# Gated mix of segment attention and SwiGLU: the logit fills of a quad in its own three visits, and pair loads issued 25 slots ahead from GpSimd's queue

## The chip, the cores and the metric

The kernel runs on one core of one Trainium2 chip. The metric is the device time of one execution in microseconds. A run of it was timed three times before the change, and one further execution was profiled; times inside the kernel are from that profile and count from the start of its span.

## The reference

The program mixes two branches over the same input x, 2048 rows of 640. Branch A is attention in 4 segments of 512 rows with 32 heads of 20 elements: causal softmax inside a segment, plus a read of a memory (the sum over the earlier segments of phi(k) times v), mixed per head by sigmoid(beta), and projected by wo. Branch B is a SwiGLU feed-forward with 1728 hidden columns. A gate per row mixes the two.

```
for s in range(4):                       # segments of 512 rows
    logits = einsum("bhqd,bhkd->bhqk", q[s], k[s]) * scale + causal_mask
    a_dot  = softmax(logits) @ v[s]
    a_mem  = (phi(q[s]) @ M) / (phi(q[s]) @ z + 1e-6)
    o      = sigmoid(beta) * a_mem + (1 - sigmoid(beta)) * a_dot
    M, z   = M + phi(k[s])^T @ v[s],  z + sum(phi(k[s]))
a = concat(o) @ wo
b = (silu(x @ w1) * (x @ w3)) @ w2
g = sigmoid(x @ gate_w)
return g * a + (1 - g) * b
```

The change is inside the softmax attention, in `logits` and what is needed to subtract each row's maximum.

## The kernel before

**How the attention is tiled.** Two neighbouring heads are a pair, two pairs (four heads) a quad. There are 4 segments x 32 heads = 128 heads, so 64 pairs and 32 quads. Queries and keys, split into a high and a low part so that fp32 precision is kept, are stored to DRAM (`qkd`), 60 rows for each head. `load_pair` (line 540) brings a pair back into one of four buffers `qk` (pair p uses buffer p % 4), each head by a DMA of 240 KB (line 549), head 0 in partitions 0 to 59, head 1 in 64 to 123. Rows 60 and 61 of each head are left for the maxima.

**Two passes over the logits.** A quad's logits are computed twice. The first pass (`s_fill`, line 564) has queries on the output's partitions; PE writes a bank of PSUM for each head of a pair, and DVE reduces each bank to row maxima in the tile `m` (line 579). The work of a quad is cut into five fills, numbered by the table `S_FILL`; fill 3 is the one whose bank holds a block of both pairs, fills 0 and 1 belong to the first pair, 2 and 4 to the second. Each table entry is (pair, block of queries, column in the bank):

```
    S_FILL = (((0, 3, 0),), ((0, 2, 0), (0, 0, 384)), ((1, 3, 0),), ((0, 1, 0), (1, 1, 256)), ((1, 2, 0), (1, 0, 384)))
    T_FILL = (((0, 0, 0),), ((0, 1, 0), (0, 3, 384)), ((0, 2, 0), (1, 2, 256)), ((1, 0, 0),), ((1, 1, 0), (1, 3, 384)))
```

`max_rows` (line 583) turns a quad's maxima into rows: ACT copies them (`ns`, line 139, and `nh`, line 140), DVE subtracts (line 141) and transposes them into `mr` (line 590), and four small DMAs from POOL's queue write `mr` into rows 60 and 61 of the four heads (line 595), those of the first pair ahead of those of the second. The second pass (`t_fill`, line 597) then computes the logits with keys on the partitions and 62 rows, so that the maxima are subtracted by the matmul itself; ACT takes the exponential (line 613) and POOL clears what lies above the diagonal (line 617). Fills t0 and t1 read the first pair, t2 both pairs, t3 and t4 the second pair. `pv_quad` (line 622) multiplies by v (line 627).

**Slots and visits.** The rest of the program (projections, feed-forward, output projection) is a stream of matmuls, woven with the attention by hand: `attention` (line 718) counts 40 slots for each quad, and between two slots as much of the stream is issued as its share asks for. At three slots of an iteration, named by `VISITS`, the fills are issued; an entry (kind, q, fill) of iteration m works on quad m - q. A visit at slot 5 of the next iteration is slot 45 counted from this one. `after(n, f)` runs f at the n-th slot from now. The second pass and the PV of a quad run in the next iteration and the one behind it.

**Who sets the order.** The order of PE is the program's own. On the other engines a scheduler orders the instructions, mostly as the program has them; calls wrapped in `here` stay where they are. An engine takes its instructions in order: one that waits for a semaphore holds up what is behind it on that engine, and a DMA's issue is such an instruction. Pair loads are issued by ACT, the maxima's DMAs by POOL, weights mostly by SP. POOL also takes part in splitting weights (W) and hidden tiles (ht), line 116.

Of the kernel before, what the change touches and what calls it, by code (L numbers as in the profile page):

```python
# [8 lines left out]
F32 = mybir.dt.float32  # L9
# [18 lines left out]
RH, LEAD = 3 * DH, 20  # L28
# [9 lines left out]
def gated_mix(ctx: ExitStack, tc: tile.TileContext, xT, wqk, wv, w13, w2, w2h, wo, beta, out):  # L38
    nc = tc.nc
# [6 lines left out]
    qkd = [dp.tile([3 * D, 2, L], F32, name=f"qkd{c}") for c in range(NSEG)]  # L46
# [54 lines left out]
    here = tc.keep_in_program_order  # L101
# [34 lines left out]
    def split_psum(dst, src, name, pin=lambda ins: ins):  # L136

        hi = bank_tile(name)[:, :src.shape[-1]]
        pin(nc.scalar.copy(dst[:, 0], src))
        nc.scalar.copy(hi, dst[:, 0].bitcast(F32))  # L140
        nc.vector.tensor_sub(dst[:, 1], src, hi)
# [301 lines left out]
    def job_read(c):  # L443
        return 5.6, memory_read(c)
# [95 lines left out]
    def load_pair(p):  # L540

        j = 2 * p
        c, h = divmod(j, H)
        t = qk[p % NST]
        for mb in {DH * h // P, (DH * h + 2 * DH - 1) // P}:
            assert ("q", c, mb) in stored and ("k", c, mb) in stored
        assert ("v", c, 3) in stored
        for i in range(2):
            here(nc.scalar.dma_start(t[64 * i:64 * i + RH].bitcast(F32), qkd[c][RH * (h + i):RH * (h + i + 1)]))
        if h % 8 == 0:  # L550
            bank["v"] = v = vg[j // 8 % NVG]
            here(nc.sync.dma_start(v[:, :, :VG], vd[c][:, :, VE * h:VE * h + VG]))
        if p % 2 == 0:
            bank["m"] = sp.tile([P, 16], F32, tag="m", name=f"m{j}", bufs=2)
        for i in range(2):
            o = VE * (h % 8 + i)
            heads[j + i] = dict(c=c, h=h + i, v=bank["v"][:, :, o:o + 32])
        pairs[p] = dict(t=t, m=bank["m"])
# [24 lines left out]
    def max_rows(p):  # L583

        m = pairs[p]["m"]
        ns = nsT[p // 2 % 2]
        split_psum(ns.rearrange("p (a n) -> p a n", a=2), m, f"nh{p}")
        mr = sp.tile([32, P], F32, tag="mr", name="mr", bufs=1)
        for g in range(4):
            nc.vector.transpose(mr[:, 32 * g:32 * g + 32], ns[32 * g:32 * g + 32].bitcast(F32))  # L590
        for k in range(2):
            for a in range(2):
                dst = pairs[p + k]["t"][RH + a:RH + a + 65:64, 0].rearrange("h (b n) -> h b n", n=P)
                r = 16 * a + 8 * k
                after(4 + 9 * k, lambda d=dst, r=r: here(nc.gpsimd.dma_start(d, mr[r:r + 8])))  # L595

    def t_fill(m, f):

# [23 lines left out]
    def pv_quad(p):  # L622

        ps = bank_tile(f"o{p}")
        for kb, (o, n) in enumerate(PSEG):
            for i in range(4):
                nc.tensor.matmul(ps[32 * i:32 * i + 32, kb * P:], heads[2 * p + i]["v"][:, kb],  # L627
                                 pairs[p + i // 2]["P"][:, i % 2, o:o + n],
                                 start=kb == 0, stop=kb == 3, skip_group_check=True)
        ot = sp.tile([P, L], F32, tag="oq", name=f"oq{p}", bufs=1)  # L630
        nc.scalar.copy(ot, ps)  # L631
        c, h = heads[2 * p]["c"], heads[2 * p]["h"]
        nc.scalar.dma_start(od[c][h:h + 4].rearrange("h e n -> (h e) n"), ot)
        q = p // 2 % 8
        for b in OUT.get(q, ()):
            after(8, o_load, c, b)
        if q == 7:
            after(6 if c < NSEG - 1 else 2, o_sums, c)
# [63 lines left out]
    def after(n, f, *a):  # L702
        soon.append([n, f, a])

    def tick():
        for e in list(soon):
            e[0] -= 1
            if e[0] <= 0:
                soon.remove(e)
                e[1](*e[2])  # L710

    NQUAD = NJ // 4


    VISITS = {5: (("s", 0, 3), ("s", 0, 1), ("o", 2), ("t", 1, 0), ("t", 1, 1)),
              18: (("s", 0, 2), ("t", 1, 2), ("s", 0, 4)), 31: (("s", -1, 0), ("t", 1, 3), ("t", 1, 4))}

    def attention():

        for m in range(-1, NQUAD + 2):  # L720
            for n in range(40):
                if m == -1 and n < 40 - LEAD:
                    continue
                if n in VISITS:
                    yield "visit"
                    for kind, q, *f in VISITS[n]:
                        if 0 <= m - q < NQUAD:
                            if kind == "o":
                                pv_quad(2 * (m - q))
                            else:  # L730
                                (s_fill if kind == "s" else t_fill)(m - q, *f)
                    if n == 18 and 0 <= m < NQUAD:
                        after(6, max_rows, 2 * m)
                elif n in (20, 32) and m + 1 < NQUAD:
                    load_pair(2 * (m + 1) + (n == 32))
                tick()
                yield m

# [62 lines left out]
    def job_down(cs, g, last=False):  # L801
        return 2.384 * sum(3 if j < NF else 2 for j in GROUPS[g]), ffn_down(cs, GROUPS[g], plan_down(GROUPS[g]), last)

    def jobs_up(cs, g):
        return [job_up(cs, j) for j in GROUPS[g]]
# [57 lines left out]
    d = job_down(A, 2)  # L863
# [6 lines left out]
    d = job_down(A, 4)  # L870
# [7 lines left out]
    r = job_read(2)  # L878
    up = [job_up(B, 0), job_up(B, 1)]
    seg += q[:2] + [braid(chain(q[2:]), r, 2, 3, False)]  # L880
    r = 0.6 * r[0], r[1]
# [6 lines left out]
    d = job_down(B, 1)  # L888
# [5 lines left out]
    d, u = job_down(B, 3), jobs_up(B, 4)  # L894
# [3 lines left out]
    for n, (_, g) in enumerate(head):  # L898
# [7 lines left out]
        elif n == 9:  # L906
            gates()
    stores(True)
    att = attention()

    def begin():
# [5 lines left out]
    def step(run):  # L917
        d = next(run[1], None)
        if d is not None:
            for k in held:  # L920
                held[k] += d
            if not isinstance(d, float):
                stores()
                w_step()
        return d
# [3 lines left out]
    while run:  # L929
# [6 lines left out]
        if next(att, None) == "visit":  # L936

            for _ in range(4):
                if max(held.values(), default=-1) >= 0:
                    break  # L940
                d = step(run)
# [6 lines left out]
        while credit > 0:  # L948
            d = step(run)
# [63 lines left out]
```

## Time and profile before

| | |
|---|---|
| median of 3 runs | 1133.49 us (1131.36 to 1136.8) |
| the profiled execution | 1132.75 us, of which the span (first to last instruction) is 1131.0 us |
| mean granted TensorE clock over the span | 0.994 of full speed |
| matmuls of the first pass (s, line 572) | 512, 72.4 us busy |
| matmuls of the second pass (t, line 607) | 512, 59.3 us busy |
| PV matmuls (o, line 627) | 1024, 77.2 us busy |
| chain that ended last | PE 88%, DMA 6%, issue 2%, the rest 1% or less each |
| DMA in the whole span | 152.00 MB, 134 GB/s |

How to read it. PE is TensorE, PEld its weight loads, DVE VectorE, ACT ScalarE, POOL GpSimd, SP SyncE. A name with a q behind it (ACTq) is the engine's sequencer, which issues DMAs. `qk<-qkd` is an instruction that writes `qk` and reads `qkd`, buffer numbers left out; L572 is line 572. Matmuls are pipelined, so the busy time of two that overlap is counted once. The chain that ended last is followed back from the end; at each step it goes to what released the instruction. The granted clock is the share of full speed that TensorE's clock had.

### The profile page before, as it was taken

What the parts mean: (1) busy time and instruction counts of PE and PEld (TensorE: products, weight loads), DVE (VectorE), ACT (ScalarE), POOL (GpSimd) and SP (SyncE); (2) the same over time, 40 slices, a digit from 0 to 9 for tenths busy, and PEclk for the clock granted to TensorE, in tenths of its full rate; (3) what the DMA queues carried; (4) which work ended last, traced back from release to release, by engine and by line L of the source; (5) the groups of instructions that cost most, each with busy time, mean ns of one, the idle gap of its engine ahead of it and who ended that gap; (6) DMA issues with size and microseconds to landing.
All of it is one profiled execution on the core that took longest, in us unless ns stands there. A gap on an engine that the chain in (4) does not pass through costs nothing.

```text
span 1131.0 us, 19258 instructions
## 1 busy us (share of the span) xinstructions
PE 1113.1 (98%) x6953; PEld 908.2 (80%) x6953; DVE 579.0 (51%) x1718; ACT 478.9 (42%) x988; POOL 473.8 (42%) x603
## 2 busy tenths in 40 slices
PE   9999999999999999999999999999999999999998
PEld 6988777877878888888877777788768778877888
DVE  5032564445646454485233666773546655651544
ACT  6255234544343333274355634535543444344040
POOL 5053245354354354352344335534643454455140
PEclk9999999999999999999999999999999999999999
DMA  9265743234343224344376765334643333442112
GB/s 326 81 234 203 254 121 92 82 90 118 90 124 106 66 83 134 112 133 143 121 256 215 250 208 159 111 118 156 180 114 97 89 92 104 119 119 76 49 59 94
DMA packets 85168, 152.00 MB, mean 134 GB/s; under 512 B 19280, under 2 KB 32080, under 8 KB 85072
## 3 DMA queue, kind: packets, MB, share of 16 engines
q1 hardware_dynamic: 55920, 95.01, 26.3%
q10 hardware_dynamic: 16512, 45.36, 13.0%
q0 software_dynamic: 12640, 10.39, 3.4%
q8 instruction: 55, 0.90, 0.3%
q14 instruction: 41, 0.34, 0.1%
HBM read 95.25 MB, written 54.53 MB: 132 GB/s over the span
## 4 chain that ended last, share of the span: by engine, by line
PE 88%; DMA 6%; issue 2%; POOL 1%; ACT 1%; DVE 1%; SPq 0%; POOLq 0%; ACTq 0%; DVEq 0%
PE f L523 17%; PE g L261 16%; PE u L261 15%; PE o L627 6%; PE k L261 6%; PE v L372 5%; PE q L261 5%; PE op L767 5%; PE s L572 5%; DMA qk<-qkd 4%; PE t L607 4%; PE nd L339 1%; PE pm L426 1%; POOL W L116 1%; PE pkt L411 1%
## 5 line engine op out<-in xcount | busy, mean ns | idle before, releaser
L579 DVE CUSTOM_DVE_ANT_0 junk<-s,mask 128x128 bf16<-128x128 f32 (+3 forms) x512 | 251.1, 490 | 139.3 <-PE s L572 103.7
L116 POOL TENSOR_TENSOR W<-wr,W 128x640 fp32r<-128x640 f32 (+1 forms) x126 | 197.5, 1573 | 229.4 <-ACT W L115 186.0
L261 PE MATMUL g<-X,W 128*128 128x512 f32 x840 | 213.2, 400 | 0.0
L613 ACT ACTIVATE P<-t 128x512 f32<-128x512 f32 (+1 forms) x384 | 171.9, 536 | 94.8 <-PE t L607 94.6
L617 POOL TENSOR_SCALAR_AFFINE_SELECT P<-P 128x256 f32<-128x256 f32 (+1 forms) x192 | 94.2, 498 | 268.5 <-ACT P L613 267.2
L523 PE MATMUL f<-W,ht 128*128 128x320 f32 x1312 | 204.6, 314 | 0.3 <-POOL W L116 0.3
L523 PEld LDWEIGHTS f<-W,ht 128*128 128x128 f32 x1312 | 195.9, 190 | 4.6 <-POOL W L116 0.6
L261 PE MATMUL u<-X,W 128*128 128x512 f32 x780 | 199.0, 400 | 0.0
L261 PEld LDWEIGHTS g<-X,W 128*128 128x128 f32 x840 | 155.3, 189 | 36.9
L261 PEld LDWEIGHTS u<-X,W 128*128 128x128 f32 x780 | 143.7, 188 | 34.4 <-issue 0.2
L115 ACT CAST W<-wr 128x640 fp32r<-128x640 f32 (+1 forms) x133 | 95.6, 730 | 92.2 <-PE u L261 31.4
L531 DVE SCALAR_TENSOR_TENSOR acc<-f,cgate,acc 128x320 f32<-128x320 f32 x128 | 69.5, 549 | 45.3 <-PE f L523 44.8
L595 POOL DMA_DIRECT2D qk<-mr x128 | 70.7, 554 | 50.9 <-DVE mr L590 44.1
L116 POOL TENSOR_TENSOR ht<-ft,ht 128x512 fp32r<-128x512 f32 x52 | 67.2, 1292 | 55.3 <-ACT ht L115 55.0
L492 DVE SCALAR_TENSOR_TENSOR fu<-ft,g 128x512 f32<-128x512 f32 x52 | 35.7, 687 | 88.3 <-ACT ft L491 75.1
L572 PE MATMUL s<-qk 60*128 60x128 f32 (+3 forms) x512 | 72.4, 347 | 7.2 <-DMA qk<-qkd 6.1
L261 PE MATMUL k<-X,W 128*128 128x512 f32 x300 | 78.1, 408 | 0.0
L627 PE MATMUL o<-P,vg 128*32 128x512 f32 (+3 forms) x1024 | 77.2, 443 | 0.0
L261 PE MATMUL q<-X,W 128*128 128x512 f32 x300 | 75.2, 401 | 1.2 <-DVE X L116 0.6
L767 PE MATMUL op<-W,oT 128*128 128x320 f32 x480 | 74.7, 312 | 0.0
L631 ACT COPY oq<-o 128x512 f32<-128x512 f32 x32 | 18.8, 587 | 127.4 <-PE o L627 127.4
L767 PEld LDWEIGHTS op<-W,oT 128*128 128x128 f32 x480 | 71.2, 189 | 1.3
(105 smaller groups left out, 1107.3 us busy)
## 6 DMA issues: line engine op xcount, KB each, us to landing
qk<-qkd ACTq DMA_DIRECT2D x128, 240.0 KB
wr<-in_w_dram SPq DMA_DIRECT2D x80, 320.0 KB
qkd<-qs SPq DMA_DIRECT2D x20, 512.0 KB
qkd<-ks SPq DMA_DIRECT2D x20, 512.0 KB
od<-oq ACTq DMA_DIRECT2D x32, 256.0 KB
wr<-in_wo_dram SPq DMA_DIRECT2D x20, 320.0 KB
vg<-vd SPq DMA_DIRECT2D x16, 336.0 KB
xr<-in_xT_dram SPq DMA_DIRECT2D x20, 256.0 KB
```

The source lines that it names most:

```text
L115: pin(nc.scalar.copy(dst[:, 0], src))
L116: (lo or nc.gpsimd.tensor_sub)(dst[:, 1], src, dst[:, 0].bitcast(F32))
L261: nc.tensor.matmul(ps, w[:, a, kb * P:(kb + 1) * P], x[:, b, kb, :], start=n == 0, stop=n == 14)
L523: nc.tensor.matmul(ps[:, :320], a, b, start=n == 0, stop=n == len(ms) - 1)
L531: nc.vector.scalar_tensor_tensor(dst, ps[:, :320], cgate[:, c, lb:lb + 1], dst, op0=ALU.mult, op1=ALU.add)
L572: nc.tensor.matmul(ps[i][:, o:o + w], q[:, qb * P:(qb + 1) * P], key[:, :w], start=n == 0, stop=n == len(todo) - 1, skip_group_check=True)
L579: nc.vector.tensor_tensor_reduce(out=junk[:, :w], in0=ps[i][:, o:o + w], in1=mask[:, L - w:], scale=1.0, scalar=-3.0e38, op0=ALU.add, op1= ...
L595: after(4 + 9 * k, lambda d=dst, r=r: here(nc.gpsimd.dma_start(d, mr[r:r + 8])))
L613: last["exp"] = nc.scalar.activation(pairs[2 * m + k]["P"][:, i, o:o + n], ps[i][:, b:b + n], AF.Exp, scale=SCALE)
L617: nc.gpsimd.affine_select(d, d, pattern=[[0, 2], [0, n], [1, P]], base=0, channel_multiplier=-1, compare_op=ALU.is_ge, fill=0.0)
L627: nc.tensor.matmul(ps[32 * i:32 * i + 32, kb * P:], heads[2 * p + i]["v"][:, kb], pairs[p + i // 2]["P"][:, i % 2, o:o + n], start=kb == 0 ...
L767: nc.tensor.matmul(ps[:, :320], oT[0][:, qb % 2, a, kb * P:(kb + 1) * P], ws[kb][:, b, 320 * hf:320 * hf + 320], start=n == 0, stop=n == 14)
```

## The change

Three things are changed, all in the order of the attention.

1. The table `VISITS`: the visits stand at slots 5, 17 and 29 (before: 5, 18, 31). A quad's first pass is now within its own iteration: fills 0 and 1 at 5, fills 2 and 4 at 17, fill 3 at 29. Before, fill 0 of the next quad stood at 31, and fill 3 with fill 1 at 5.
2. `max_rows` is called 4 slots behind the visit at 29 (before: 6 behind the one at 18), and its DMAs follow at 3 and 11 slots (before: 4 and 13).
3. The pair loads are issued by GpSimd's queue instead of ScalarE's, the first at slot 20 as before, the second at slot 36 (34 in the iteration that comes ahead of the first quad; before: 32). The tile is written as fp32r instead of through a view as fp32.

```
-            here(nc.scalar.dma_start(t[64 * i:64 * i + RH].bitcast(F32), qkd[c][RH * (h + i):RH * (h + i + 1)]))
+            here(nc.gpsimd.dma_start(t[64 * i:64 * i + RH], qkd[c][RH * (h + i):RH * (h + i + 1)]))
...
-                after(4 + 9 * k, lambda d=dst, r=r: here(nc.gpsimd.dma_start(d, mr[r:r + 8])))
+                after(3 + 8 * k, lambda d=dst, r=r: here(nc.gpsimd.dma_start(d, mr[r:r + 8])))
...
-    VISITS = {5: (("s", 0, 3), ("s", 0, 1), ("o", 2), ("t", 1, 0), ("t", 1, 1)),
-              18: (("s", 0, 2), ("t", 1, 2), ("s", 0, 4)), 31: (("s", -1, 0), ("t", 1, 3), ("t", 1, 4))}
+    VISITS = {5: (("s", 0, 0), ("s", 0, 1), ("o", 2), ("t", 1, 0), ("t", 1, 1)),
+              17: (("s", 0, 2), ("t", 1, 2), ("s", 0, 4)), 29: (("s", 0, 3), ("t", 1, 3), ("t", 1, 4))}
...
-                    if n == 18 and 0 <= m < NQUAD:
-                        after(6, max_rows, 2 * m)
-                elif n in (20, 32) and m + 1 < NQUAD:
-                    load_pair(2 * (m + 1) + (n == 32))
+                    if n == 29 and 0 <= m < NQUAD:
+                        after(4, max_rows, 2 * m)
+                elif n in ((20, 34) if m < 0 else (20, 36)) and m + 1 < NQUAD:
+                    load_pair(2 * (m + 1) + (n > 20))
```

The order on the engines, with buffer numbers: `s17_3_0` is quad 17, fill 3, head 0 of the pair; `t16_4_1` is fill 4 of the second pass of quad 16; `P33` holds the probabilities of pair 33, the second of quad 16; x15 means 15 alike. First PE, from the last visit of iteration 17 to the first fill of the next visit; before:

```order
L261 MATMUL u2_1_7363<-X2_5223,W80_6780 128x512 x6
L572 MATMUL s18_0_0_7370<-qk0_86 128x512
L572 MATMUL s18_0_1_7371<-qk0_86 128x512
L607 MATMUL t16_3_0_7378<-qk1_87 128x512
L607 MATMUL t16_4_1_7386<-qk1_87 128x128
L261 MATMUL u2_1_7363<-X2_5223,W80_6780 128x512 x9
L261 MATMUL g3_1_7411<-X3_5427,W79_6694 128x512 x6
L572 MATMUL s18_3_0_7418<-qk0_86 128x256
```

and now:

```order
L261 MATMUL g2_1_7303<-X2_5209,W79_6671 128x512 x12
L572 MATMUL s17_3_0_7330<-qk2_88 128x256
L572 MATMUL s17_3_1_7331<-qk2_88 128x256
L607 MATMUL t16_3_0_7344<-qk1_87 128x512
L607 MATMUL t16_4_1_7352<-qk1_87 128x128
L261 MATMUL g2_1_7303<-X2_5209,W79_6671 128x512 x3
L261 MATMUL u2_1_7378<-X2_5209,W80_6770 128x512 x15
L261 MATMUL g3_1_7401<-X3_5417,W79_6671 128x512 x6
L572 MATMUL s18_0_0_7410<-qk0_86 128x512
```

The visit begins 9 matmuls of the stream earlier, holds the last fill of quad 17 in place of the first of quad 18, and 24 matmuls of line 261 stand between it and the next visit.

Next ACT, at the copy of quad 17's maxima (`ns1`); before it stands ahead of the exponentials of t3 and t4 of quad 16:

```order
L115 CAST W84_7321<-wr84_7042 128x640
L115 CAST ht3_0_7247<-ft3_0_7248 128x512
L139 CAST ns1_99<-m68_6987 128x16
L140 COPY nh34_7326<-ns1_99 128x16
L491 ACTIVATE ft2_1_7359<-g2_1_7317 128x512
L613 ACTIVATE P33_7278<-t16_3_0_7378 128x512
```

and now behind them:

```order
L115 CAST ht3_0_7233<-ft3_0_7234 128x512
L613 ACTIVATE P33_7264<-t16_3_0_7344 128x512
L613 ACTIVATE P33_7264<-t16_3_1_7345 128x512
L613 ACTIVATE P33_7264<-t16_4_0_7351 128x512
L613 ACTIVATE P33_7264<-t16_4_1_7352 128x512
L491 ACTIVATE ft2_1_7365<-g2_1_7303 128x512
L139 CAST ns1_99<-m68_6973 128x16
L140 COPY nh34_7369<-ns1_99 128x16
```

Last POOL at the same place, where the maxima of quad 17 (`qk2` and `qk3` are its pairs) are sent; before:

```order
L116 TENSOR_TENSOR W84_7321<-wr84_7042,W84_7321 128x640
L116 TENSOR_TENSOR ht3_0_7247<-ft3_0_7248,ht3_0_7247 128x512
L595 DMA qk2_88<-mr_7330 2x4x128 x2
L617 AFFINE_SELECT P33_7278<-P33_7278 128x2x128 x2
L617 AFFINE_SELECT P33_7278<-P33_7278 128x2x256
L595 DMA qk3_89<-mr_7330 2x4x128 x2
```

and now, with the two loads of quad 18 (`qk0` and `qk1`):

```order
L549 DMA qk0_86<-qkd2_70 60x1024 x2
L116 TENSOR_TENSOR W84_7307<-wr84_7017,W84_7307 128x640
L116 TENSOR_TENSOR ht3_0_7233<-ft3_0_7234,ht3_0_7233 128x512
L617 AFFINE_SELECT P33_7264<-P33_7264 128x2x128 x2
L617 AFFINE_SELECT P33_7264<-P33_7264 128x2x256
L595 DMA qk2_88<-mr_7373 2x4x128 x2
L549 DMA qk1_87<-qkd2_70 60x1024 x2
L116 TENSOR_TENSOR ht2_1_7364<-ft2_1_7365,ht2_1_7364 128x512
L595 DMA qk3_89<-mr_7373 2x4x128 x2
```

The first pair's maxima have moved behind the selects of t3 and t4, the second load stands behind them, and the second pair's maxima behind that load.

## The prediction

> **What bounds the kernel now.** I read the page's first part, then the waits of PE alone, then windows, then the timeline of one quad.
>
> ```profile
> PE 1113.1 (98%) x6953; PEld 908.2 (80%) x6953; DVE 579.0 (51%) x1718; ACT 478.9 (42%) x988; POOL 473.8 (42%) x603
> ```
>
> PE is busy for 1113.1 of 1131.0 us, and its order is written by hand, so the change can win only what PE waits for, and what PE runs slowly. No other engine is near a bound. The waits of PE (engine, line, releaser: us, times, longest):
>
> ```profile
> PE s L572 <- DMA qk<-qkd: 6.1, 8, 1.5
> PE pkt L411 <- DVE pk L295: 1.9, 1, 1.9
> PE nd L339 <- DVE pq L295: 1.2, 1, 1.2
> ```
>
> A third of PE's 18 us without work is one thing: a logit fill (s, line 572) that waits for its pair's load. The other waits have nothing to do with the change. No row of the list names a wait for the maxima's transfer (qk<-mr, line 595): today it is always in time. Three of these waits on the timeline of PE (start, us, line, out<-in, times; in brackets the idle time before):
>
> ```profile
> 774.71 0.46 PE L572 MATMUL s<-qk 60*128 60x512 f32 x1 [1.26 <-DMA qk<-qkd]
> 826.01 0.62 PE L572 MATMUL s<-qk 60*128 60x256 f32 x5 [1.33 <-DMA qk<-qkd]
> 916.04 0.46 PE L572 MATMUL s<-qk 60*128 60x512 f32 x1 [1.45 <-DMA qk<-qkd]
> ```
>
> And five windows (us; PE, PEld, DVE, ACT, POOL busy; granted clock, DMA share, GB/s):
>
> ```profile
> 650.00:830.00 180.00, 173.16 (x1160) 134.82 (x1160) 112.10 (x390) 80.52 (x173) 84.85 (x117) 0.97 0.51 153
> 830.00:1045.00 215.00, 213.46 (x1390) 169.24 (x1383) 115.71 (x364) 91.28 (x190) 102.88 (x129) 1.00 0.35 102
> 775.50:779.00 3.50, 3.50 (x15) 3.43 (x14) 0.41 (x2) 2.22 (x5) 2.04 (x5) 0.53 0.80 222
> 826.60:829.10 2.50, 2.50 (x17) 0.77 (x20) 2.13 (x10) 0.00 (x0) 0.00 (x0) 0.56 0.00 0
> 916.90:919.50 2.60, 2.60 (x13) 2.15 (x12) 1.74 (x5) 1.75 (x4) 1.81 (x4) 1.00 0.62 178
> ```
>
> The loss sits in 650 to 830, where DMA is busiest. Right after the waits that ended at 774.7 and 826.0 the granted clock is 0.53 and 0.56: (1 - 0.53) x 3.5 = 1.6 us and (1 - 0.56) x 2.5 = 1.1 us of PE time, which the waits list doesn't count. The wait of 1.45 us at 916 has no such tail (1.00), so a tail comes sometimes.
>
> **Part 1: the loads, 25 slots ahead.** One quad in the stretch (start, us, engine, line, out<-in, times; idle before):
>
> ```profile
> 679.52 0.50 PE L572 MATMUL s<-qk 60*128 60x512 f32 x2
> 680.42 2.37 PE L261 MATMUL u<-X,W 128*128 128x512 f32 x9
> 687.57 0.50 PE L572 MATMUL s<-qk 60*128 60x512 f32 x2
> 688.97 0.42 ACTq L549 DMA_DIRECT2D qk<-qkd  x1
> 689.31 1.09 ACT L613 ACTIVATE P<-t 128x512 f32<-128x512 f32 x2
> 692.14 0.56 PE L572 MATMUL s<-qk 60*128 60x256 f32 x3
> 693.28 0.61 PE L572 MATMUL s<-qk 60*128 60x256 f32 x5 [0.57 <-DMA qk<-qkd]
> 696.11 0.73 PE L607 MATMUL t<-qk 62*128 62x512 f32 x6
> ```
>
> Visits stand at 679.52 (slot 18), 687.57 (slot 31) and 692.14 (slot 5 of the next). From 680.42 to 687.57 are 13 slots: 0.55 us each. The second pair's load is issued at 688.97 and ends PE's wait at 693.28, 4.3 us later. In the change the first load keeps slot 20, but its first reader moves from slot 31 to slot 45: 25 slots, 13.7 us and the visit at 29. The second moves to slot 36, with its first reader in the visit at 57: 21 slots, 11.5 us, and the visit at 45. Against 4.3 us (half as much again in a crowd) both have room, so I take all of the 6.1 us, and the two tails: 6.1 + 1.6 + 1.1 = **8.8 us** less. If PE's other waits grow by what it gains, as little as 4 is left; that is my lower end.
>
> **Part 2: by GpSimd's queue.** It adds 128 issues to POOL and takes 128 from ACT. Rows of lines 595 and 549 (ns: min/median/max of an issue), POOL's group of another load (line 680) and its landing on the page (us), a wait of POOL, and one row of the timeline:
>
> ```profile
> L595 POOL DMA_DIRECT2D qk<-mr x128: 537/553/584, 141.3 to 1022.2; - x128
> L549 ACTq DMA_DIRECT2D qk<-qkd x128: 321/364/1394, 113.8 to 992.8; - x128
> L680 POOL DMA_DIRECT2D gm<-gd x12 | 6.9, 575 | 0.2
> gm<-gd POOLq DMA_DIRECT2D x12, 320.0 KB, 4.1
> POOL P L617 <- ACT P L613: 267.2, 125, 14.2
> 681.30 0.64 POOL L617 TENSOR_SCALAR_AFFINE_SELECT P<-P 128x512 f32<-128x512 f32 x1 [0.23 <-ACT P L613]
> ```
>
> An issue from POOL costs 553 ns for 4 KB and 575 ns for 320 KB (line 680), so it doesn't go by size: 128 x 0.56 = 72 us, which takes POOL from 474 to 546 of 1131 us. POOL idles 267 us for ACT ahead of its selects alone, so it has the time: 0. ACT's queue loses 128 x 0.36 = 46 us, also 0. A 320 KB load by this queue lands in 4.1 us (median), like today's. On POOL the first load stands behind the selects of t2, which end at 681.94, where slot 20 is: it is issued no later than now. The second stands behind the two qk<-mr of the first pair, and behind it stand the second pair's qk<-mr: these land last of all, which I weigh below. The destination is now written as fp32r, as qk<-mr's is: no row shows that on 240 KB. Between nothing and twice 4.3 us I take nothing, by the row of line 680; twice would still land within 13.7 us.
>
> [...]
>
> **Part 3: fill 3 goes last, fill 0 first.** The fills are the same 512 matmuls, and PE makes as many visits, but one. What moves is the maxima. Their last fill was in the visit at 18, and t0 of the next quad reads them after slot 45. Now the last fill is in the visit at 29. The chain that follows, as it stands today (quad 17):
>
> ```profile
> 684.51 0.20 ACT L139 CAST ns<-m 128x16 fp32r<-128x16 f32 x1
> 684.74 0.18 ACT L140 COPY nh<-ns 128x16 f32<-128x16 f32 x1
> 684.95 0.17 DVE L141 TENSOR_TENSOR ns<-m,nh 128x16 fp32r<-128x16 f32 x1 [0.79 <-ACT nh L140]
> 685.16 0.84 DVE L590 STREAM_TRANSPOSE mr<-ns 32x32 f32<-32x32 f32 x4
> 686.40 1.16 POOL L595 DMA_DIRECT2D qk<-mr  x2
> ```
>
> And the groups of the reductions ahead of it (mean ns behind the comma):
>
> ```profile
> L579 DVE CUSTOM_DVE_ANT_0 junk<-s,mask 128x256 bf16<-128x256 f32 x128 | 54.3, 424 | 47.8 <-PE s L572 41.2 <-DVE m L579 0.5
> L579 DVE DVE_READ_ACCUMULATOR2_ANT m<- 128x1 f32 x512 | 42.6, 83 | 0.0
> ```
>
> Need, from the start of the visit at 29: fill 3's reductions on DVE, 0.6 + 4 x (0.424 + 0.083) = 2.6 us; but ACT puts the maxima's copy behind the four exponentials of t3 and t4, which today end at 690.40, 2.8 us after their visit began. Then 684.51 to 686.00, 1.5 us, so 4.4. POOL's two issues: the second starts 0.6 later. Then the landing (first all 128, then the 28 between 700 and 860):
>
> ```profile
> DMA to landing us min/median/max: 1.6/2.5/7.3
> DMA to landing us min/median/max: 1.6/3.0/7.3
> ```
>
> 4.4 + 0.6 + 3.0 = **8.0 us** in the crowded stretch, 7.5 at the median of all. Room, by the changed order at quad 17: 24 matmuls of line 261 stand between, and two visits' parts. Their rates (the first row from the chain of waits, the others from the timeline):
>
> ```profile
> 315.20 3.47 PE u L261 x15
> 338.84 0.50 PE L572 MATMUL s<-qk 60*128 60x512 f32 x2
> 339.75 2.35 PE L261 MATMUL g<-X,W 128*128 128x512 f32 x9
> 346.91 0.73 PE L572 MATMUL s<-qk 60*128 60x256 f32 x8
> 349.86 0.73 PE L607 MATMUL t<-qk 62*128 62x512 f32 x6
> ```
>
> 24 x 3.47 / 15 = 5.6, the visit 0.9 (338.84 to 339.75), the next visit's fills and its PV 2.95 (346.91 to 349.86): **9.4 us**. The margin is 1.4 us at the stretch's median, and a landing of over 4.4 us eats it. A quad takes 40 x 0.55 + 0.9 + 0.9 + 2.95 = 26.8 us here, so about ten of them lie from 650 to 930, where the loads wait now. I can't read off which land late, so I bound it: nothing, if the landings get shorter because pair loads no longer run beside them; ten times 1.5 us, if each does as the worse ones do now. I take three quads with 1 us each, **3.0 us**, near the lower end, since the median lands in time.
>
> Second pair: issued some 2 us behind the first, needed by t2, a visit later. No cost.
>
> **The sum.** The profiled execution took 1132.75 us (its span 1131.0, and 1.75 around it), 0.7 below the median of the runs, 1133.49. 1132.75 - 8.8 + 3.0 = 1126.95; from the median, 1133.49 - 5.8 = **1127.7 us**.
>
> The tails of low clock are a choice of mine. [...]
>
> **Rivals.** 0.5% of the time, 5.7 us, is about what can be told from no change here.
>
> 1. Forecast: load waits and their tails go, a few waits for qk<-mr come. 1124 to 1130.5, chance 0.60, of which 0.37 lies under 1127.8.
> 2. The wait for the load becomes one for the maxima: about nine of the ten quads 1 us late, 1133.49 - 8.8 + 9 = 1133.7 (1130.5 to 1137). For it: the margin is of the size of the spread of the landings. Against: the median of all landings, 2.5, leaves 1.9. Chance 0.18.
> 3. Nothing of it: POOL runs its queue in order, and loads behind its conversions and a wait for mr come as late as now: 1133.5 (1131 to 1136). For: the second load stands behind qk<-mr. Against: 11.5 us of lead. Chance 0.07.
> 4. Slower: the same place as 2, but where the margin is overrun by 1.5 us in all ten quads, each wait is long enough for a tail of low clock (1.35 us, the mean of the two) in half of them: 1133.49 - 8.8 + 15 + 6.8 = 1146 (1139 to 1150). It decides from landings of about 5.9 us on (4.4 + 1.5); the longest is 7.3 now. Chance 0.12.
> 5. Better: no wait for qk<-mr, and the pq waits go with ACT's shorter queue: 1133.49 - 8.8 - 1.2 = 1123.5. Chance 0.03.
>
> Faster by over 0.5%: 0.37 + 0.03 = 0.40; within: 0.23 + 0.17 + 0.07 = 0.47; slower: 0.01 + 0.12 = 0.13. The range is 1123 to 1137: it leaves out case 4 and a little of 1 and 5. The forecast's own is 1124 to 1130.5.
>
> **What would show it.** PE's waits for qk<-qkd near 0, and full clock after 775 and 826: part 1 right. Rows of PE t, line 607, waiting for qk<-mr, between 650 and 930: part 3; their sum against 3.0 us decides between 1, 2 and 4. POOL at about 546 us busy, with line 549's issues near 0.56 us: part 2. Wrong would be: waits for qk<-qkd that stay, or W or ht (POOL, line 116) appearing among PE's releasers.

## The result and the profile after

| | before | after |
|---|---|---|
| median of the runs | 1132.6 us (1131.36 to 1136.8, 4 runs) | 1118.65 us (1117.9 to 1119.14, 4 runs) |
| span of the profiled execution | 1131.0 us | 1116.7 us |
| mean granted clock | 0.994 | 1.000 |

The ratio is 0.987, 95% interval 0.9843 to 0.9897: the change makes the kernel 14 us faster. The forecast was 1127.7, with a range from 1123.0 to 1137.0: the sign was right, the gain more than twice as large, and the time below the range. First the page, busy us of each engine:

```profile
PE 1104.2 (99%) x6953; PEld 902.2 (81%) x6953; DVE 577.0 (52%) x1718; ACT 475.4 (43%) x988; POOL 544.8 (49%) x731
```

PE's busy time fell by 8.9 us with the same 6953 matmuls, and its idle time from 17.9 to 12.5 us. POOL went from 473.8 to 544.8, where 546 was forecast. The five longest waits of PE after the change (engine, line, releaser: us, times, longest):

```profile
PE warm L851 <- DVE zero L848: 1.3, 1, 1.3
PE nd L339 <- DVE pq L295: 1.1, 1, 1.1
PE t L607 <- DMA qk<-mr: 1.0, 2, 0.6
PE s L572 <- DVE pq L295: 1.0, 1, 1.0
PE pkt L411 <- DVE pk L295: 0.9, 1, 0.9
```

No row of the list names qk<-qkd: the 6.1 us of waiting for loads are gone. The maxima are waited for twice, 1.0 us in all. The busy time fell by 8.9 us because PE's clock no longer falls, and because fewer matmuls run alone. Fill 0 of quad 22 in both, first before, in the visit at 31 (start, us, engine, line, out<-in, times; idle before):

```profile
772.98 0.47 PE L572 MATMUL s<-qk 60*128 60x512 f32 x1 [0.41 <-DMA qk<-qkd]
```

The row that followed it, at 774.71, is shown in the prediction. After the change, with fill 1 in the visit at 5:

```profile
772.60 0.74 PE L572 MATMUL s<-qk 60*128 60x512 f32 x6
```

Before, fill 0 of head 0 and of head 1 stand in two rows, 1.7 us apart; where both loads are there, a pair of them is one row of 0.50 us (679.52, in the prediction), and the two run side by side, head 0 from partitions 0 to 59 and head 1 from 64 to 123: at the median head 1 starts 3 ns behind head 0, and a matmul of line 261, over all 128 partitions, 232 ns behind the one before it. A load that comes late for one head costs this overlap as well, 0.47 + 0.46 us in place of 0.50, and that counts as busy time. Of the 512 pairs of logit matmuls (256 in each pass), head 1 starts over 0.1 us behind head 0 in 35 before and in 3 after.

The clock is read from windows of 3.41 us (PE, PEld, DVE, ACT, POOL busy; granted clock; DMA). Of the kernel before, two windows ahead of a low stretch, each with the stretch behind it, and one that none follows:

```profile
567.49:570.90 3.41, 1.47 (x9) 0.94 (x9) 1.98 (x3) 1.98 (x4) 1.87 (x2) 1.00 0.82 244
570.90:574.31 3.41, 3.41 (x11) 2.64 (x10) 0.00 (x1) 1.31 (x2) 1.57 (x1) 0.50 1.02 344
...
823.49:826.90 3.41, 2.08 (x15) 1.13 (x18) 1.30 (x7) 0.62 (x1) 1.26 (x1) 1.00 0.27 80
826.90:830.31 3.41, 3.41 (x28) 1.27 (x24) 2.16 (x10) 0.00 (x0) 0.00 (x0) 0.50 0.00 0
912.23:915.64 3.41, 2.36 (x12) 1.49 (x10) 3.31 (x12) 1.61 (x5) 0.00 (x0) 1.00 0.68 163
```

The recorded clock is exactly half in four stretches of 3.41 us before (from 570.9, 659.6, 775.7 and 826.9) and in none after, up to PE's last matmul. By the clock each costs 3.41 / 2 = 1.71 us where PE is busy throughout, 6.8 us in all at most; by the matmuls somewhat less: 13 of line 523 run in the 3.41 us from 775.68 and 24 in the 3.41 us behind them, which makes 3.41 x (1 - 13 / 24) = 1.6 us (an estimate). The accounts below take the 1.71. The four stretches begin at whole multiples of 3.413 us from each other (26, 34 and 15 of them), so the windows lie on a fixed grid. In the window ahead of each, PE idled: 3.41 - 1.47 = 1.94 us ahead of 570.90 and 1.33 us ahead of 826.90; with 1.05 us (912.23) nothing followed. The windows with most idle time after the change:

```profile
645.37:648.78 3.41, 2.43 (x18) 1.63 (x17) 2.95 (x8) 1.93 (x6) 2.71 (x4) 1.00 0.97 350
652.19:655.60 3.41, 2.28 (x17) 1.53 (x16) 2.46 (x8) 3.41 (x8) 1.80 (x2) 1.00 1.01 366
655.60:659.01 3.41, 3.41 (x21) 3.04 (x22) 2.62 (x14) 0.97 (x4) 1.72 (x4) 1.00 0.73 248
```

1.13 us of idle time (652.19) is the most in any, and the clock stays at 1.00. So the span's 14.3 us are 5.4 of idle time, 6.8 of low clock, and 2.1 of busy time at full clock. I read these 2.1 as the lost overlap of the two heads; the experiments test that. The size is blurred by the start: ahead of the first clock record, at 4.3 us before and at 7.1 after, the first matmuls run slowly (the warm-up's take 609 to 634 ns each there, and 379 to 407 right behind it), so the profile after the change has 2.8 us more of slow running. Counted from PE's 41st matmul on, with the low stretches at half their busy time, the busy time fell by 3.1 us.

### The profile page after: what moved, and what is told of

The parts are those of the page before. It is cut to its first block, busy times and chain, and to the rows that moved or that the text cites. A ratio compares the mean times of both kernels' runs of the same rounds, so it can differ in the third digit from the quotient of the medians.

```text
span 1116.7 us, 19428 instructions
## 1 busy us (share of the span) xinstructions
PE 1104.2 (99%) x6953; PEld 902.2 (81%) x6953; DVE 577.0 (52%) x1718; ACT 475.4 (43%) x988; POOL 544.8 (49%) x731
## 4 chain that ended last, share of the span: by engine, by line
PE 89%; issue 3%; DVE 2%; POOL 2%; DMA 2%; ACT 1%; SPq 0%; POOLq 0%; ACTq 0%; DVEq 0%
PE f L523 17%; PE g L261 16%; PE u L261 15%; PE q L261 6%; PE o L627 6%; PE k L261 6%; PE v L372 5%; PE s L572 5%; PE op L767 5%; PE t L607 4%; PE nd L339 2%; PE pm L426 1%; DMA qk<-mr 1%; DVE junk L579 1%; POOL W L116 1%
## 5 line engine op out<-in xcount | busy, mean ns | idle before, releaser
L579 DVE CUSTOM_DVE_ANT_0 junk<-s,mask 128x384 bf16<-128x384 f32 (+3 forms) x512 | 251.0, 490 | 138.0 <-PE s L572 102.9
L595 POOL DMA_DIRECT2D qk<-mr x128 | 73.6, 577 | 31.7 <-DVE mr L590 25.8
L372 PE MATMUL v<-W,X 128*128 128x320 f32 (+1 forms) x480 | 71.8, 311 | 0.0
```

The lines of the kernel that those rows point to most:

```text
L372: nc.tensor.matmul(ps[:, :n1 - n0], x[:, a, kb, lb * P:(lb + 1) * P], wvt[kb][:, b, n0:n1], start=n == 0, stop=n == 14)
L579: nc.vector.tensor_tensor_reduce(out=junk[:, :w], in0=ps[i][:, o:o + w], in1=mask[:, L - w:], scale=1.0, scalar=-3.0e38, op0=ALU.add, op1= ...
L595: after(3 + 8 * k, lambda d=dst, r=r: here(nc.gpsimd.dma_start(d, mr[r:r + 8])))
```

## The experiments

Nine runs follow: seven other kernels, and the two kernels of the change once more. "Before" in the ratios is the old kernel, timed beside each run on the same chip.

**The queue, with the change's order.**

```diff
-            here(nc.gpsimd.dma_start(t[64 * i:64 * i + RH], qkd[c][RH * (h + i):RH * (h + i + 1)]))
+            here(nc.scalar.dma_start(t[64 * i:64 * i + RH].bitcast(F32), qkd[c][RH * (h + i):RH * (h + i + 1)]))
```

> The changed kernel, with the pair loads back on ScalarE's queue at the same slots. If the lead of the loads is what counts, PE waits for no load (qk<-qkd under 0.5 us in all) and the time is the changed kernel's, 1118.5 us, within 2. If GpSimd's queue is what helps (an issue that ScalarE's exponentials no longer hold up), waits for qk<-qkd of 3 us or more come back and the time is 1122 or more. If the queue costs something (73 us more of POOL's time), this is faster, 1117 or less.

Measured: 1119.13 us (1118.59 to 1119.56), ratio to before 0.9878 (0.9856 to 0.99). No wait for a load, 0.6 us for the maxima, no low clock. The first theory holds: by these two times, 1118.65 and 1119.13, GpSimd's queue neither helps nor costs anything here. The type of the destination, fp32r or fp32, went back with the queue, so it costs nothing here either.

**The queue alone.** The kernel before, with line 549 as the change has it and nothing else.

> The kernel before, with the pair loads issued from GpSimd's queue at the old slots 20 and 32, nothing else changed. If the lead counts, PE still waits about 6 us for qk<-qkd (4 to 9) and the time stays at 1132.6, within 3. If the queue counts, these waits fall under 2 us and the time is 1124 or less. If POOL holds the loads up behind its selects, the waits grow past 9 us and the time is 1137 or more.

Measured: 1196.45 us, ratio 1.0562 (1.0534 to 1.059). The third theory, and far beyond its number. The row of PE's waits:

```profile
PE s L572 <- DMA qk<-qkd: 36.9, 35, 4.5
```

35 waits in place of 8. The first load of a quad shows why; before the change on ACT's timeline (quad 20's load), then here on POOL's (quad 19's), then what PE makes of the second (t2's matmuls start at 725.20 before and at 734.35 here):

```profile
725.63 0.38 ACT L613 ACTIVATE P<-t 128x256 f32<-128x256 f32 x1 [0.83 <-PE t L607]
725.68 0.32 ACTq L549 DMA_DIRECT2D qk<-qkd  x1
```

```profile
735.80 0.64 POOL L617 TENSOR_SCALAR_AFFINE_SELECT P<-P 128x512 f32<-128x512 f32 x1 [1.57 <-ACT P L613]
736.39 1.11 POOL L549 DMA_DIRECT2D qk<-qkd  x2
```

```profile
734.35 0.40 PE L607 MATMUL t<-qk 62*128 62x256 f32 x4
...
739.96 0.49 PE L572 MATMUL s<-qk 60*128 60x512 f32 x1
740.61 0.50 PE L572 MATMUL s<-qk 60*128 60x512 f32 x1 [0.16 <-DMA qk<-qkd]
```

On ACT's queue the load leaves 0.48 us behind the start of t2, which frees its buffer; on POOL it stands behind the select, which waits for ACT's exponentials, and leaves 2.04 us behind. Over all quads the medians are 0.48 and 2.04 us for the first load, and 0.71 and 3.64 us behind t3 for the second. So POOL's queue does make the loads later, by 1.6 and 2.9 us, and only the change's lead hides it: uncovered it costs 63 us. The transfer itself isn't slower: from issue to landing the loads take 3.7 us here at the median, against the 4.3 us timed in the prediction. The last two rows show why the 30.8 us of added waits cost so much more. The list counts 0.16 us of idle time, but head 1 starts 0.65 us behind head 0, beside which it otherwise runs. Against the kernel before, the span is 62.2 us longer: 33.8 of idle time, some 19 to 20 of low clock (13 stretches of 3.41 or 6.83 us, 16 windows against 4), and 8 to 9 of busy time at full clock. Head 1 is over 0.1 us late in 111 pairs here, against 35.

**The lead without the late fill 3.**

```diff
-    VISITS = {5: (("s", 0, 3), ("s", 0, 1), ("o", 2), ("t", 1, 0), ("t", 1, 1)),
-              18: (("s", 0, 2), ("t", 1, 2), ("s", 0, 4)), 31: (("s", -1, 0), ("t", 1, 3), ("t", 1, 4))}
+    VISITS = {5: (("s", 0, 0), ("s", 0, 1), ("o", 2), ("t", 1, 0), ("t", 1, 1)),
+              18: (("s", 0, 2), ("s", 0, 3), ("t", 1, 2), ("s", 0, 4)), 31: (("t", 1, 3), ("t", 1, 4))}
```

> The kernel before with its slots and queue; fill 0 stands in its own quad's visit at 5, fill 3 in the one at 18, so that the first reader of the first load is 25 slots behind it, and the maxima are complete at 18 as before. If the load waits with all that hangs on them are the whole gain, both they and the waits for qk<-mr are near 0, and the time is 1117 to 1120. If the late fill 3 and the new slots bring something of their own, it stays at 1122 to 1128. If eight logit matmuls in one visit press DVE or the banks, new waits of PE for DVE m show, and the time is 1128 or more.

Measured: 1148.9 us, ratio 1.0151 (1.0126 to 1.0176). No wait of PE for a load or for the maxima is left, and still it is slower than before: it doesn't tell the first two theories apart, and the third holds. The visit at 18 of quad 18, and DVE in it:

```profile
708.16 0.41 PE L607 MATMUL t<-qk 62*128 62x256 f32 x4
708.41 0.97 PE L572 MATMUL s<-qk 60*128 60x384 f32 x4
708.88 0.29 PEld L572 LDWEIGHTS s<-qk 60*128 60x128 f32 x3 [0.40 <-DVE m L579]
```

```profile
708.12 0.69 DVE L579 CUSTOM_DVE_ANT_0 junk<-s,mask 128x512 bf16<-128x512 f32 x1 [1.07 <-PE s L572]
708.74 0.08 DVE L579 DVE_READ_ACCUMULATOR2_ANT m<- 128x1 f32 x1
```

Fill 4's four matmuls take 0.97 us; in the kernel before they take 0.40 (visit at 724.86). Head 1's weights load only when a reduction of an earlier bank has ended (708.74 + 0.08, then 708.88), while head 0's matmul runs alone. PE counts as busy nearly throughout. The visit lasts 1.72 us, from 707.59 to the stream's next matmul at 709.31; its parts side by side would make some 1.1 us, by the 0.90 of the visit at 724.86 before and 0.22 for fill 3 (an estimate). Against the kernel before, the span is 16.2 us longer: 8.9 of idle time, 10.7 of busy time at full clock, and 3.4 less of low clock. So two heads one after the other do cost time that no list of waits shows, and eight logit banks in one visit (six of the first pass, two of t2) were too many here. Since the visit itself became dear, this run can't say what the load waits alone are worth.

**The kernel before, again.**

> The kernel before, unchanged, for a second profile. In the first the granted clock is 0.5 in four stretches of exactly 3.41 us, at 570.6, 659.3, 775.4 and 826.6, which lie 26, 34 and 15 times 3.413 us apart. If the clock is set on a grid of such windows by how long PE idled in the window before, low stretches are again 3.41 us each and on one grid, each behind a window with about 1.3 us of idle time or more, but not at the same places: 2 to 5 of them, and the time moves by 1.7 us with each. If they belong to fixed places of the program, the same four show.

(Its times of low clock count from the first working instruction, 0.3 us later than the zero of the rows shown here.) Measured: 1132.4 us, ratio 0.9996 (0.998 to 1.0011). Windows of its profile:

```profile
568.32:571.73 3.41, 1.59 (x10) 1.13 (x9) 1.56 (x3) 2.31 (x4) 1.55 (x1) 1.00 1.00 312
571.73:575.14 3.41, 3.41 (x20) 2.98 (x19) 0.00 (x0) 0.94 (x3) 1.56 (x1) 1.00 0.97 333
769.71:773.12 3.41, 1.20 (x7) 0.66 (x5) 0.15 (x1) 0.53 (x1) 1.16 (x2) 1.00 1.00 332
773.12:776.53 3.41, 2.84 (x12) 2.52 (x13) 1.25 (x4) 2.01 (x4) 0.42 (x1) 0.50 0.64 167
```

Two stretches: 6.83 us from 773.1, two windows long, and 3.41 us from 827.7, again on one grid; I had expected each to last 3.41 us. The waits for pk and pq at 570 and 659, behind which the clock fell in the first profile, are there again (1.8 and 1.4 us), with no low clock behind them: 1.82 us of idle time at 568.32, and 1.00 in the next window. So the windows of low clock come and go between two executions of one kernel, and the fixed places are refuted. That the place of a wait on the grid decides is not shown: this wait lay whole in one window. Its waits for loads are 6.3 us in 10.

**The order of the fills alone.** The kernel before with its queue, load slots and visits at 5, 18 and 31:

```diff
-    VISITS = {5: (("s", 0, 3), ("s", 0, 1), ("o", 2), ("t", 1, 0), ("t", 1, 1)),
-              18: (("s", 0, 2), ("t", 1, 2), ("s", 0, 4)), 31: (("s", -1, 0), ("t", 1, 3), ("t", 1, 4))}
+    VISITS = {5: (("s", 0, 0), ("s", 0, 1), ("o", 2), ("t", 1, 0), ("t", 1, 1)),
+              18: (("s", 0, 2), ("t", 1, 2), ("s", 0, 4)), 31: (("s", 0, 3), ("t", 1, 3), ("t", 1, 4))}
...
-                    if n == 18 and 0 <= m < NQUAD:
-                        after(6, max_rows, 2 * m)
+                    if n == 31 and 0 <= m < NQUAD:
+                        after(4, max_rows, 2 * m)
```

(with the maxima's DMAs at 3 and 11 slots, as the change has them).

> The kernel before with the changed order of fills alone: fill 0 in its own quad's visit at 5, fill 3 in the last visit, and the maxima after that; visits at 5, 18 and 31, loads at 20 and 32 on ScalarE's queue as before. If the order of the fills is what removes the load waits, PE waits for no load (under 0.5 us). The last visit stands two slots later than in the changed kernel, so the maxima have 1.1 us less: by the margins in its trace 4 to 5 us of waits for qk<-mr, none over 1.3 us: 1121 to 1126 with no low clock. If the new slots and the later second load are needed, load waits of 3 us or more stay and the time is 1127 or more. If the margin is used up more sharply than the one trace shows, the waits for qk<-mr are over 9 us and the time is 1130 or more.

Measured: 1133.24 us (1130.0 to 1135.17, 12 runs), ratio 1.001 (0.9995 to 1.0025): no gain at all. The row of PE's waits that matters:

```profile
PE t L607 <- DMA qk<-mr: 8.7, 7, 2.2
```

There is no wait for a load, as the first theory said, but the maxima are late by 8.7 us in 7 waits, where 4 to 5 us were expected, and one stretch of low clock is back, from 1029.6. The time is in the third theory's range, the waits just short of its 9 us: the margin is used up more sharply than one trace shows. The profiled execution is the fastest of the twelve, with a granted clock of 0.998; the others have 0.994 to 0.998. This is rival 2 of the prediction, at the old slots: the wait for the loads turned into one for the maxima, for the same time. The first experiment has the same queue and order with the visits at 17 and 29 and the second load at 36, and takes 14 us less.

**The maxima later**, to price such waits: the changed kernel with 8 and with 11 slots for the 4.

```diff
-                        after(4, max_rows, 2 * m)
+                        after(8, max_rows, 2 * m)
```

> The changed kernel with the maxima's copy called 8 slots behind the visit at 29 instead of 4, so that they land some 2.2 us later in the dense stretches. By the margins in the changed kernel's trace the waits for qk<-mr are 9 to 14 us in 8 to 12 quads, 5 of them 1.3 us or longer. If a wait costs its idle time alone, 1118.7 + 10 = 1129. If PE's idle time in a 3.41 us window also halves the clock in the next, some 3 to 6 such windows come on top, 5 to 10 us: 1134 to 1139. If the margin is wider than it looks (the copy moves less than 2.2 us), under 1124.

> The same with 11 slots, some 3.85 us later. By the margins 30 to 40 us of waits for qk<-mr in about 19 quads, 12 of them over 1.3 us. Idle time alone: 1118.7 + 35 = 1154. With a halved window of 1.7 us behind each long wait: 12 to 20 of them, 20 to 34 us more, 1174 to 1188.

Measured: 1141.74 us (1137.8 to 1144.53) and 1162.06 us (1160.56 to 1162.62), ratios 1.0081 (1.0059 to 1.0103) and 1.0261 (1.0241 to 1.0281). The rows of the waits, of the first and of the second:

```profile
PE t L607 <- DMA qk<-mr: 15.4, 10, 3.5
```

```profile
PE t L607 <- DMA qk<-mr: 29.9, 19, 7.3
```

Low clock costs 8.2 us in the first (five windows) and 10.1 us in the second (seven, in one of which PE runs nothing): half of what PE is busy in them. Against the changed kernel the spans are 22.6 and 42.9 us longer; 14.9 and 31.2 of that is idle time, 8.2 and 10.1 low clock, and -0.5 and 1.6 busy time at full clock. So idle time alone is refuted in both. Both forecasts were off: the first has 15.4 us of waits for 9 to 14 and lies above its 1134 to 1139; in the second I had expected 12 to 20 low windows and 1174 or more, but a wait of 1.3 us or longer is not always followed by one. These waits hold up both heads at once, so little overlap can be lost: head 1 is late in 5 pairs in the first and in 8 in the second, and where the second's 1.6 us come from is open.

**More room for the maxima.** The order of the first experiment, with the visits at 5, 16 and 27 and the second load at 34.

```diff
-              17: (("s", 0, 2), ("t", 1, 2), ("s", 0, 4)), 29: (("s", 0, 3), ("t", 1, 3), ("t", 1, 4))}
+              16: (("s", 0, 2), ("t", 1, 2), ("s", 0, 4)), 27: (("s", 0, 3), ("t", 1, 3), ("t", 1, 4))}
...
```

> The changed order of fills with the visits at 5, 16 and 27, the loads on ScalarE's queue at 20 and 34. The maxima get 1.1 us more room than in the changed kernel, and the loads 22 and 25 slots. If the margin of the maxima still costs something in the changed kernel, no wait for qk<-mr is left and the time is 1117 to 1118.5; the trace shows 1.0 us to win at most. If the slots of the visits set other waits (for pk, pq and X, about 1 us each), these change places, and one of 1.3 us or more may bring a low clock window: up to 1122. If the selects and exponentials of t3 and t4 come too early for the loads, waits for qk<-qkd return: over 1122.

> The changed kernel, unchanged, for a second profile. If low clock windows come only behind windows of 1.2 us of idle time or more, and no wait of that length is left, there is none in this profile either, and the runs lie within 2 us of each other, 1117.5 to 1119.5. If the windows of low clock come and go by chance whatever the waits, one to four appear here, and runs spread by 1.7 us steps.

Measured: 1119.91 us (1116.37 to 1120.5), ratio 0.989 (0.9867 to 0.9913), and for the changed kernel again 1118.36 us (1118.16 to 1118.64), ratio 0.9882 (0.9859 to 0.9906). At the median more room wins nothing: one wait for the maxima of 1.1 us is left, and others moved, as the second theory has it. One, for X, grew from 0.8 to 1.8 us, and low clock follows it (the other such stretch is at the start, from 10.0):

```profile
498.11:501.52 3.41, 1.66 (x13) 1.10 (x13) 2.73 (x9) 3.14 (x7) 1.93 (x2) 1.00 0.19 72
501.52:504.93 3.41, 3.41 (x10) 2.67 (x9) 0.49 (x4) 1.99 (x6) 1.02 (x2) 0.50 0.34 101
```

The changed kernel's second profile again has no low clock, no wait for a load, and 0.5 us of waiting for the maxima. Where low clock stays away the earlier visits may even win: the one run of the six with a clock of 1.000 took 1116.37 us.

The changed kernel's eight runs lie within 1.3 us; the old kernel's 17 runs beside the first experiments lie within 7.9 us (1129.2 to 1137.13). Low windows that come and go explain most of that, since the record has the granted clock of every run: of the old kernel's 57 runs here, the 27 at 0.994 or 0.995 took 1133.6 us on average, the 23 at 0.997 or 0.998 took 1130.4, and the only one at 1.000 took 1127.44. The changed kernel's eight, at 0.999 or 1.000, took 1118.5. So some 9 of the 14 us are there without any low clock, and some 5 are low clock that the old kernel has in most runs and the new one hardly at all.

## Why the prediction was right about the mechanism and short by more than half

| term, us | predicted | from profile to profile |
|---|---|---|
| idle time, waits for loads | -6.1 | -6.1 |
| low clock behind those waits | -2.7 | -3.4 |
| busy time at full clock (two heads one after the other, and the start) | not counted | -2.1 |
| low clock behind the waits for pk and pq | kept | -3.4 |
| the wait for pk | kept | -1.0 |
| waits for the maxima | +3.0 | +1.0 |
| other waits (X, m, gm) | none | +0.7 |
| sum | -5.8 | -14.3 |

**Part 1, the lead: right, its price too low.** All waits for loads went, and the order of the fills alone takes them away. The leads came out near the forecast, 12.3 and 11.0 us at the median (8.3 and 7.0 at the shortest), against 4.1 us for a landing at the median and 8.7 at the longest. The step that failed is the price, "6.1 + 1.6 + 1.1 = 8.8". Read from windows cut by eye, a tail came out as 1.6 or 1.1 us; by the recorded clock each is a window of 3.41 us at half speed, 1.71 us. And the list of waits leaves out what a wait for one head's load costs in overlap. The prediction put that at nothing without a reason. Counted from PE's 41st matmul on, as above, PE is busy at full clock for 1091.0 to 1091.1 us in three profiles without load waits (the changed kernel twice, and with its loads on ScalarE's queue), for 1094.3 and 1095.3 in the two of the kernel before, with 8 and 10 waits, and for 1102.7 with 35 waits in the experiment on the queue alone: 0.33 to 0.42 us for each wait. The other kernels without load waits, the one with the fat visit at 18 aside, lie at 1090.2 to 1093.2, so the size is known to a us or two and not better; that lateness of one head is what costs rests on the rows of 774.71 and 740.61 and on the count of late pairs. So 6.1 us of waits were worth 6.1 + 3.4 + 3.1 = 12.6 us. The same pair of profiles taken again gives as much and more: from 1131.2 to 1116.2, the span falls by 15.0 us.

**The waits that were to stay.** I kept the waits for pk and pq with all that hangs on them. They stayed, but that for pk shrank from 1.9 to 0.9 us, and no low clock followed either. That is 4.4 us of the gain, and not all of it is owed to the change: the second profile of the kernel before has no low clock there either, so the 3.4 us are in part luck of the first profile. In that one, in turn, the load waits brought three windows instead of two and more idle time, and its span is 0.2 us longer. Over all runs low clock makes some 5 of the 14 us, where the prediction had 2.7; the 6.8 of the first profile are more than the old kernel's usual share. Why the wait for pk is shorter isn't settled: it is 0.7 to 1.0 us in the four profiles with the last visit at 29 or 27, 2.0 at the old slots (the order of the fills alone), 2.2 with the maxima 4 slots later, and gone with them 7 slots later. What is shown is that after the change no window reaches the idle time behind which the clock falls, in two profiles of two.

**Part 2, the queue: the cost was right, a sentence was wrong.** POOL's busy time and the issues (a median of 548 ns for 0.56 us) came as worked out, and the queue costs nothing in the changed kernel (1118.65 us, 1119.13 with ScalarE's). But "it is issued no later than now" was wrong: it is issued 1.6 us later behind t2, since the select it stands behind waits for ACT. What hides that is the lead, and without it the price is 63 us. Rival 3 was given the time of no change; at the old slots it would have been a large loss.

**Part 3, the maxima: the mechanism right, the term too large.** The chain was forecast at 8.0 us in the dense stretch. The medians of its parts over quads 16 to 28 are 3.0 us from fill 3 to the copy, 2.1 to the DMA and 2.6 to the landing, 7.7 in all. The room was the error: I used quad 17's 9.4 us for ten quads. It is 10.6 there, with a wait of 0.7 us in it, and 11.1 us at the median of those quads, so the usual margin is some 2.7 us and not 1.4. Two quads waited 0.5 us each, not three 1 us; one of them is the last quad, at 1013, outside the stretch. The dense stretch holds 13 quads and not ten, since a quad takes 22.7 us there and not 26.8, and four of the 13 have 0.7 us of margin or less. How near rival 2 was, the order at the old slots shows: with the last visit at 31 in place of 29 the room, waits left out, is 9.7 us at the median in place of 11.0, the chain 7.6 in place of 7.7, and PE waits 8.7 us in place of 1.0.

**The range** was built with low clock as a price of rival 4 alone. On the better side it let go only the two tails seen at the load waits, so that 1123 was its end.

## What to carry to other kernels

Price a wait of PE by three things, its idle time, the matmuls that lose their partner beside them, and the clock in the window that follows; here 6.1 us in the list of waits were worth about 12.6. When work is moved so that one transfer has time, look for the chain that now ends last, and take its room quad by quad: here the reordering alone gained nothing, and with the visits one and two slots earlier and the second load four slots later it gained 14 us. GpSimd's queue, by which the loads left 1.6 and 2.9 us later, cost nothing here with the lead (1118.65 us against 1119.13) and 63 us without it, so test the queue and the lead apart.

## What the runs showed of the hardware

**The clock falls by windows.** In all eleven profiles the low stretches are whole multiples of 3.413 us long and lie on one grid within an execution; only the last, which the end of the record cuts, is not. I laid that grid over all profiles and took PE's idle time in each window at full clock, up to PE's end: of 16 windows with 1.95 us or more, all are followed by half clock; of 33 with 1.20 to 1.95, 17; of some 3540 with less than 1.20, none (the two bounds are drawn from these same windows). So 1.2 to 1.95 us of idle time in a window were enough about half of the time. What decides in that band (the idle time alone does not: 1.92 us went without, 1.20 did not) is open.

The longest wait shows the same window by window (the experiment with 11 slots):

```profile
776.48:779.89 3.41, 0.00 (x0) 0.00 (x0) 1.07 (x4) 0.37 (x1) 3.10 (x4) 1.00 0.91 313
779.89:783.30 3.41, 0.00 (x0) 0.00 (x0) 0.00 (x0) 0.00 (x0) 0.00 (x0) 0.50 0.91 271
783.30:786.72 3.42, 3.14 (x14) 2.95 (x15) 1.73 (x8) 1.74 (x5) 1.55 (x3) 0.50 0.20 72
786.72:790.13 3.41, 3.41 (x15) 3.41 (x14) 0.00 (x0) 0.53 (x1) 0.13 (x1) 0.50 0.63 144
790.13:793.54 3.41, 3.41 (x28) 3.04 (x26) 1.59 (x7) 2.10 (x5) 0.36 (x1) 1.00 0.00 0
```

PE idles through two windows and the clock is half in the second, where nothing runs; it stays so in the next two, in one of which PE is busy for 3.14 of 3.42 us at that clock, and returns behind a full one.
